# Reordering the start of a fused attention and maxout kernel: loads, casts and copies of batches 0 and 1

## The chip, the cores and the metric

The kernel runs on one core of a Trainium2 chip. The metric is the device time of one execution in microseconds (us); the span that the profile shows is the same execution from first to last instruction, about 1.8 us shorter. PE is TensorE, PEld its weight loads, DVE is VectorE, ACT is ScalarE, POOL is GpSimd, and SPq is the queue from which SyncE issues DMAs. The granted clock is the share of full speed that the profile shows as granted to TensorE (0.978 on the mean in the profiled execution of before).

## The reference, cut to what matters

```python
B, H, S, Ns, D = 8, 8, 512, 32, 64        # x: B,H,S,D   state: B,H,Ns,D
scores = scale * x @ state^T ;  a  = softmax(scores)  ;  xread = a  @ state    # per batch and head
scores2 = scale * state @ x^T;  a2 = softmax(scores2) ;  sread = a2 @ x
X = concat([xread, sread], axis=2) -> [B*(S+Ns), 512]
out = maximum(X @ w1, X @ w2) @ w_out      # w1, w2: 512x1024, w_out: 1024x512
```

The kernel uses two identities. First, max(h1, h2) @ Wo = relu(h1 - h2) @ Wo + h2 @ Wo, so it needs W1 - W2 and the product W2 Wo. Second, xread @ W = a @ (S @ W), so it multiplies the 32 rows of state S by the weights once per batch ("S W", in the buffer `swt`). Layer one of a batch is then `aT` times `swt`.

## The kernel before

Everything of batch 0, and of batch 1 up to its layer one, is a hand-ordered list of calls. From batch 1 on a loop runs layer one and layer two of batch b, and slips the preparation of batch b+1 in between as "fillers". The parts that matter (cuts are marked):

```python
load_x(0)
for ch in range(2): ...                      # W2, Wo
load_w(w1f, moe_w1, 0); load_w(w1f, moe_w1, 1)
load_x(1)
...
def warm_up(n):                              # matmuls on a zero tile, results unused
    p = bank()
    for k in range(n):
        nc.tensor.matmul(p, warm[:, 0:128], warm, start=(k == 0), stop=(k == n - 1))
...
def u_norm(b, g, mul):                       # sum, reciprocal, a = e * 1/sum   (mul: the engine of the last)
    nc.vector.tensor_reduce(d["es"][:, g], ...)
    nc.vector.reciprocal(d["er"][:, g], d["es"][:, g])
    mul.tensor_mul(d["a"][:, g]..., d["e"][:, g], d["er"]...)
def d_at(b):                                 # batches 2..7: aT by DMA transpose
    nc.sync.dma_start_transpose(out=AT[b]..., in_=st[b]["a"]...)
def u_at(b, eng):                            # batches 0, 1: aT on TensorE, copied out of PSUM by eng
    ...
# ---- the list (cut) ----
w_cast(w1b, w1f, 0)                          # W1a (first 512 columns): halves on DVE and ACT
w_sub(0); w_sub(1)                           # W1a - W2a on GpSimd
for i in range(4): w_wo(3, i)                # last group of W2 Wo, copies to wcat within
u_sw(0, 0); u_sw(0, 2)                       # S W of batch 0
l1(0, {}, range(0, 4))
...
u_sc(1, 0, nc.vector)                        # batch 1: scores, exp, norm
u_sc(1, 1, nc.gpsimd)
cast_x(2)                                    # GpSimd
...
u_at(1, "V")
...
one_ring()                                   # PSUM: 4 + 4 buffers become one ring of 8
for b in range(1, B):
    if b + 2 < B: cast_x(b + 2); ...         # GpSimd
    l1(b, fill)
    ...
    l2(b, fill)                              # fillers: ... u_sw(n), d_at(n), d_xt(n + 1), ...
```

The softmax here doesn't subtract the row's maximum and nothing guards it: scores larger than these inputs give would overflow.

## Time and profile before

| | before |
|---|---|
| time, the three executions known when the prediction was made | 156.42 us median, 154.05 to 156.94 |
| profiled execution | 153.81 us, span 152.0, mean granted clock 0.978 |
| layer one of batch 0 starts | 26.77 us |
| scores of batch 1 start | 36.21 us |
| layer one of batch 1 starts | 43.86 us |
| each later batch | 13.96 us |
| PE busy | 142.4 of 152.0 us |

The table says how to read the rest: 108 of the 152 us are a steady march of PE after 43.86 us, and the change works on what lies ahead of it. The prediction below shows the page's rows and the chain. Two more views turn out to matter. The first is the table of windows (window, its length, busy us and instructions of each engine, the granted clock, the DMA share, GB/s):

```profile
8.00:16.00 8.00, 6.86 (x101) 4.96 (x102) 5.88 (x12) 4.65 (x6) 3.04 (x3) 0.57 1.05 389
42.00:50.00 8.00, 7.17 (x55) 3.33 (x54) 4.88 (x9) 3.88 (x9) 2.84 (x3) 1.00 0.88 229
```

In this execution the granted clock was 0.57 from 8 to 16 us. The second is the tile view of `aT`, with the time from the issue of its DMA transpose to its landing, for batches 2 to 7:

```profile
DMA to landing us min/median/max: 3.2/3.3/3.8
```

### The profile page before, as it was taken

What the parts mean: (1) busy time and instruction counts of PE and PEld (TensorE: products, weight loads), DVE (VectorE), ACT (ScalarE), POOL (GpSimd) and SP (SyncE); (2) the same over time, 40 slices, a digit from 0 to 9 for tenths busy, and PEclk for the clock granted to TensorE, in tenths of its full rate; (3) what the DMA queues carried; (4) which work ended last, traced back from release to release, by engine and by line L of the source; (5) the groups of instructions that cost most, each with busy time, mean ns of one, the idle gap of its engine ahead of it and who ended that gap; (6) DMA issues with size and microseconds to landing.
All of it is one profiled execution on the core that took longest, in us unless ns stands there. A gap on an engine that the chain in (4) does not pass through costs nothing.

```text
span 152.0 us, 3031 instructions
## 1 busy us (share of the span) xinstructions
PE 142.4 (94%) x1255; PEld 68.7 (45%) x1255; DVE 85.5 (56%) x151; ACT 75.4 (50%) x126; POOL 44.4 (29%) x44
## 2 busy tenths in 40 slices
PE   6669997999979999999999999999999999999990
PEld 1247462434424544543454445345434534664460
DVE  5366769715965757556654657555566546631120
ACT  3047354845864846374754648463747226621010
POOL 3025329993470460073009003600500050000000
PEclk9965999999999999999999999999999999999999
DMA  4999999939969759939992986593089023602423
GB/s 102 356 393 387 387 383 324 283 80 209 226 129 304 263 107 266 285 107 170 280 297 51 197 296 232 99 246 144 2 107 341 39 35 49 265 0 68 140 100 113
DMA packets 37934, 29.89 MB, mean 197 GB/s; under 512 B 24864, under 2 KB 33312, under 8 KB 37024
## 3 DMA queue, kind: packets, MB, share of 16 engines
q1 hardware_dynamic: 37776, 29.56, 67.9%
q8 instruction: 10, 0.16, 0.4%
q10 hardware_dynamic: 144, 0.13, 0.3%
q14 instruction: 4, 0.03, 0.1%
HBM read 15.20 MB, written 8.91 MB: 159 GB/s over the span
## 4 chain that ended last, share of the span: by engine, by line
PE 84%; DVE 7%; DMA 4%; ACT 2%; issue 0%; SPq 0%
PE acc L326 34%; PE ps L311 18%; PE acc L322 10%; DMA xf<-in_x_dram 4%; PE ps L283 3%; PE ps L221 2%; PE ps L370 2%; PE acc L380 2%; PE acc L415 2%; DVE w1b L70 2%; PE ps L244 2%; PE ps L404 2%; PE acc L360 1%; PE ps L203 1%; PE acc L378 1%; PE ps L136 1%
## 5 line engine op out<-in xcount | busy, mean ns | idle before, releaser
L326 PE MATMUL acc<-wo,r 128*128 128x512 bf16 x248 | 58.9, 379 | 0.0
L326 PEld LDWEIGHTS <-r 128*128 128x128 bf16 x248 | 23.9, 98 | 28.8 <-issue 0.6
L231 POOL TENSOR_TENSOR a<-e,er 128x512 bf16<-128x512 bf16 x13 | 13.4, 1048 | 63.1 <-ACT e L224 29.9
L301 DVE TENSOR_SCALAR r<-ps 128x512 bf16<-128x512 f32 x32 | 22.1, 691 | 16.4 <-PE ps L311 16.3
L311 PE MATMUL ps<-aT,swt 128*128 128x512 bf16 x128 | 29.1, 379 | 1.0 <-ACT sread_t L68 0.8
L70 DVE COPY ob<-acc 128x512 f32<-128x512 f32 (+1 forms) x17 | 11.4, 671 | 27.4 <-PE acc L326 27.0
L299 ACT ACTIVATE r<-ps 128x512 bf16<-128x512 f32 x32 | 19.2, 601 | 8.5 <-PE ps L311 7.9
L68 ACT CAST swt<-ps 128x512 bf16<-128x512 f32 x24 | 12.9, 592 | 14.2 <-PE ps L283 14.2
L311 PEld LDWEIGHTS <-swt 128*128 128x128 bf16 x128 | 12.1, 98 | 15.4 <-DVE swt L70 1.5
L322 PE MATMUL acc<-swt,aT 128*128 128x512 bf16 x62 | 18.1, 381 | 0.0
L68 ACT COPY ob<-acc 128x512 f32<-128x512 f32 (+1 forms) x16 | 9.2, 576 | 15.9 <-PE acc L326 10.9
L70 DVE CAST swt<-ps 128x512 bf16<-128x512 f32 x24 | 15.2, 679 | 1.9 <-PE ps L283 1.9
L72 POOL CAST xp<-xf 128x2048 bf16<-128x2048 f32 (+1 forms) x8 | 14.1, 1761 | 6.3 <-DMA xf<-in_x_dram 6.3
L224 ACT ACTIVATE e<-ps 128x512 bf16<-128x512 f32 x16 | 8.8, 595 | 14.1 <-PE ps L221 14.1
L68 ACT CAST xc<-xf 128x1024 bf16<-128x1024 f32 x14 | 13.9, 1051 | 0.0
L228 DVE TENSOR_REDUCE es<-e 128x16 f32<-128x512 bf16 x16 | 10.6, 662 | 1.6 <-ACT e L224 1.6
L389 POOL TENSOR_TENSOR wcat<-w1f,w2f 128x1024 bf16<-128x1024 f32 x4 | 10.6, 2660 | 2.8 <-DMA w1f<-in_moe_w_dram 2.8
L136 PE MATMUL ps<-warm 128*128 128x512 bf16 x15 | 6.4, 567 | 1.3 <-POOL warm L122 1.3
L322 PEld LDWEIGHTS <-aT 128*128 128x128 bf16 x62 | 4.7, 98 | 6.0 <-issue 2.6
L415 PE MATMUL acc<-wo,w2t 128*128 128x512 bf16 x32 | 7.2, 379 | 0.0
L283 PE MATMUL ps<-wcat,sbd 64*32 64x512 bf16 x168 | 6.8, 380 | 0.2 <-DVE wcat L70 0.2
L221 PEld LDWEIGHTS <-xt 128*128 128x128 bf16 x128 | 5.0, 102 | 2.8 <-ACT xt L68 0.7
(68 smaller groups left out, 107.7 us busy)
## 6 DMA issues: line engine op xcount, KB each, us to landing
xf<-in_x_dram SPq DMA_DIRECT2D x8, 1024.0 KB, 8.7
out_dram<-ob SPq DMA_DIRECT2D x7, 1024.0 KB, 5.1
w2f<-in_moe_w_dram SPq DMA_DIRECT2D x2, 1024.0 KB, 10.4
wof<-in_moe_w_out_dram SPq DMA_DIRECT2D x4, 512.0 KB, 11.1
w1f<-in_moe_w_dram SPq DMA_DIRECT2D x2, 1024.0 KB, 14.3
out_dram<-ob SPq DMA_DIRECT2D x3, 256.0 KB, 2.0
out_dram<-obs SPq DMA_DIRECT2D x8, 64.0 KB, 1.7
s_f<-in_state_dram SPq DMA_DIRECT2D x1, 320.0 KB, 13.3
```

The costliest lines, as they stand in the source:

```text
L68: nc.scalar.copy(o, i)
L70: nc.vector.tensor_copy(o, i)
L72: nc.gpsimd.tensor_copy(o, i)
L228: nc.vector.tensor_reduce(d["es"][:, g], d["e"][:, g].rearrange("p i c n -> p (i c) n"), axis=mybir.AxisListType.X, op=ALU.add)
L231: mul.tensor_mul(d["a"][:, g].rearrange("p c i n -> p i c n"), d["e"][:, g], d["er"][:, g].rearrange("p (i c) -> p i c", i=4).unsqueeze(3) ...
L283: nc.tensor.matmul(pg[g][32 * i:32 * i + 32, :], sneg[gs, b, i, :] if k else sbd[gs, b, 2 * i + g, g, :], w[gs, i, ch * 512:(ch + 1) * 512 ...
L299: nc.scalar.activation(out=o, in_=p, func=ACTF.Relu)
L301: nc.vector.tensor_scalar(o, p, scalar1=0.0, scalar2=None, op0=ALU.max)
L311: nc.tensor.matmul(p, SW[b][:, g, f * 128:(f + 1) * 128], AT[b][:, g, :], start=(g == 0), stop=(g == 1))
L322: nc.tensor.matmul(OB[b][1 + c], AT[b][:, g, c * 128:(c + 1) * 128], SW[b][:, g, FF:WC], start=(g == 0), stop=False)
L326: nc.tensor.matmul(OB[b][1 + c], R[b][:, f, c * 128:(c + 1) * 128], wo[:, f, :], start=False, stop=(f == NF - 1))
L389: nc.gpsimd.tensor_sub(wcat[:, :, cs], w1f[:, :, cs], w2f[:, :, cs])
```

## The change

Its intent is to start layer one of batch 0 earlier, and with it everything behind it. x0 comes in two halves. x1 is loaded ahead of the second half of W1 ("W1b"). W1a is cast by DVE, ACT and GpSimd at once, and the subtraction W1 - W2 moves from that spot to later. S W1 of batch 0 stands right behind the matmuls of W2 Wo, with two of their copies ahead of it and two behind. More warm-up matmuls are meant to keep the clock up (from 8 to 16 us it was 0.57 in the profile of before). For the buffers, two PSUM rings of four stay to the end in place of the later ring of eight. (PSUM holds TensorE's results here, the tiles `ps` and `acc` of the matmul rows; a ring is a set of its buffers, or banks, used in turn.)

```diff
-    early = ctx.enter_context(ExitStack())
-    pools = dict(ps=early..., acc=early...)
+    pools = {k: ctx.enter_context(tc.tile_pool(name=k, bufs=4, space=bass.MemoryType.PSUM)) for k in ("ps", "acc")}
...
-    load_x(0)
+    load_x(0, 2)
...
     load_w(w1f, moe_w1, 0)
+    load_x(1)
     load_w(w1f, moe_w1, 1)
-    load_x(1)
...
-        two = b < TWO and ch < 2 and (b, ch) != (1, 0)
+        two = b < TWO and ch == 0
...
-    warm_up(5)
+    warm_up(9)
...
-    w_cast(w1b, w1f, 0)
-    w_sub(0)
-    w_sub(1)
+    for e, i in (("V", slice(0, 2)), ("A", slice(2, 3)), ("P", slice(3, 4))):
+        copy(e, w1b[:, i, 0:512], w1f[:, i, 0:512])
     for i in range(4):
         w_wo(3, i)
+    w_wo_out(0)
+    w_wo_out(1)
     u_sw(0, 0)
+    w_wo_out(2)
+    w_wo_out(3)
+    cast_x(1)
+    l1(0, {}, range(0, 4))
     u_sw(0, 2)
-    l1(0, {}, range(0, 4))
...
+    w_sub(2, nc.vector)
+    w_sub(3, nc.vector)
...
-    u_sc(1, 0, nc.vector)
-    u_sc(1, 1, nc.gpsimd)
+    u_exp(1, 0)
+    u_exp(1, 1)
+    u_norm(1, 0, nc.vector)
+    u_norm(1, 1, nc.vector)
     cast_x(2)
+    w_sub(0)
+    w_sub(1)
...
-    one_ring()
     for b in range(1, B):
```

(Cut: the order of W2 Wo's groups, of the copies between them and of batch 1's pieces.)

More of the change, by code (lines that the diff above doesn't have):

```diff
@@ L49 @@
     big = ctx.enter_context(tc.tile_pool(name="big", bufs=2))
-    early = ctx.enter_context(ExitStack())
-    pools = dict(ps=early.enter_context(tc.tile_pool(name="ps", bufs=4, space=bass.MemoryType.PSUM)),
-                 acc=early.enter_context(tc.tile_pool(name="acc", bufs=4, space=bass.MemoryType.PSUM)))
+    pools = {k: ctx.enter_context(tc.tile_pool(name=k, bufs=4, space=bass.MemoryType.PSUM)) for k in ("ps", "acc")}
     ctx.enter_context(tc.manual_schedule())
@@ L60, in acc @@
         return bank(kind="acc")
-    def one_ring():
-        early.close()
-        pools["ps"] = pools["acc"] = ctx.enter_context(tc.tile_pool(name="ring", bufs=8, space=bass.MemoryType.PSUM))
     def copy(eng, o, i):
@@ L275, in sw_mm @@
     def sw_mm(b, ch, engs="VA"):
-        pg = [bank(), bank()]
-        two = b < TWO and ch < 2 and (b, ch) != (1, 0)
+        pg = [bank(kind="acc" if ch == 2 and b > 1 else "ps") for g in range(2)]
+        two = b < TWO and ch == 0
         terms = ((sbd, w1b), (sneg, w2b)) if two else ((sbd, wcat),)
@@ L384, in moe_sread, with w_sub @@
                 nc.sync.dma_start(out=out[b * L + S:(b + 1) * L], in_=ob[32 * q:32 * q + 32, t, :])
-    def w_sub(q):
+    def w_sub(q, eng=nc.gpsimd):
         cs = slice(q * 256, (q + 1) * 256)
-        nc.gpsimd.tensor_sub(wcat[:, :, cs], w1f[:, :, cs], w2f[:, :, cs])
+        eng.tensor_sub(wcat[:, :, cs], w1f[:, :, cs], w2f[:, :, cs])
     def w_cast(o, w, ch, engs="VA"):
@@ L415, in w_wo, with w_wo_out @@
             nc.tensor.matmul(WO[i], w2t[:, i, f, :], wo[:, f, :], start=(f == 0), stop=(f == NF - 1))
-        if q == 3:
-            copy("V" if i % 2 else "A", wcat[:, i, FF:WC], WO[i])
+    def w_wo_out(i):
+        copy("V" if i % 2 else "A", wcat[:, i, FF:WC], WO[i])
     def fillers(b):
@@ L444 @@
     states(first)
-    warm_up(5)
-    cast_x(0, (("V", slice(0, 4, 2)), ("A", slice(4, 8, 2)), ("V", slice(1, 4, 2)), ("P", slice(5, 8, 2))))
+    warm_up(9)
+    cast_x(0, (("A", slice(0, 4, 2)), ("V", slice(4, 8, 2)), ("P", slice(1, 4, 2)), ("V", slice(5, 8, 2))))
     u_xt(0, 0, "V")
+    warm_up(2)
     u_xt(0, 1, "A")
     u_exp(0, 0)
+    warm_up(2)
     u_exp(0, 1)
-    w_cast(w2b, w2f, 0, "VV")
+    warm_up(3)
+    w_cast(w2b, w2f, 0, "PA")
+    u_norm(0, 0, nc.vector)
+    u_norm(0, 1, nc.vector)
+    w_t(0, 0, "A")
+    w_t(0, 1, "A")
+    u_sr(0)
     wo_cast(0, "P")
@@ L454 @@
     warm_up(1)
-    w_t(0, 0, "A")
-    w_t(0, 1, "A")
-    u_norm(0, 0, nc.vector)
-    u_sr(0)
-    u_norm(0, 1, nc.vector)
-    negate_states()
-    warm_up(3)
-    for q in range(2):
-        for i in range(4):
-            w_wo(q, i)
+    for i in range(4):
+        w_wo(0, i)
+    u_at(0, "V")
     w_cast(w2b, w2f, 1)
-    wo_cast(2, "P")
+    for i in range(4):
+        w_wo(1, i)
     w_t(1, 0, "V")
     w_t(1, 1, "A")
-    u_at(0, "V")
+    negate_states()
+    wo_cast(2, "P")
+    wo_cast(3, "P")
     u_srt(0)
-    wo_cast(3, "V")
+    warm_up(2)
     for i in range(4):
         w_wo(2, i)
-    w_cast(w1b, w1f, 0)
-    w_sub(0)
-    w_sub(1)
+    for e, i in (("V", slice(0, 2)), ("A", slice(2, 3)), ("P", slice(3, 4))):
+        copy(e, w1b[:, i, 0:512], w1f[:, i, 0:512])
     for i in range(4):
         w_wo(3, i)
+    w_wo_out(0)
+    w_wo_out(1)
     u_sw(0, 0)
+    w_wo_out(2)
+    w_wo_out(3)
+    cast_x(1)
+    l1(0, {}, range(0, 4))
     u_sw(0, 2)
-    l1(0, {}, range(0, 4))
-    for c in range(NC):
-        l2_open(0, c)
-    w_cast(w1b, w1f, 1)
     compact_x(1, 0)
@@ L487 @@
     d_xt(1)
-    cast_x(1)
-    w_sub(2)
-    w_sub(3)
+    load_x(3)
+    w_sub(2, nc.vector)
+    w_sub(3, nc.vector)
     cast_states("P", rest)
-    load_x(3)
     sT = d_states(rest)
-    l2_add(0, 0, range(0, 4))
+    for c in range(NC):
+        l2_open(0, c)
+    for c in range(NC - 1):
+        l2_add(0, c, range(0, 4))
     u_sw(0, 1)
-    for c in range(1, NC):
-        l2_add(0, c, range(0, 4))
+    l2_add(0, 3, range(0, 4))
     l1(0, {}, range(4, 8))
-    u_sc(1, 0, nc.vector)
-    u_sc(1, 1, nc.gpsimd)
+    u_exp(1, 0)
+    u_exp(1, 1)
+    u_norm(1, 0, nc.vector)
+    u_norm(1, 1, nc.vector)
     cast_x(2)
+    w_sub(0)
+    w_sub(1)
     l2_add(0, 0, range(4, 8))
     l2_close(0, 0)
-    u_sw(1, 0)
+    u_sw(1, 1)
+    u_sr(1)
     l2_add(0, 1, range(4, 8))
     l2_close(0, 1)
-    u_sw(1, 1)
-    u_sr(1)
+    u_sw(1, 0)
     compact_x(2, 0)
     compact_x(2, 1)
+    d_xt(2)
     l2_add(0, 2, range(4, 8))
@@ L513 @@
     u_at(1, "V")
+    u_sw(1, 2)
+    u_srt(1)
     l2_add(0, 3, range(4, 8))
     l2_close(0, 3)
-    d_xt(2)
-    u_sw(1, 2)
-    u_srt(1)
     l2_out(0)
-    one_ring()
     for b in range(1, B):
```

## The prediction

> **What bounds the kernel now.** I read the page's busy shares first, then the chain that ended last in order of time, then the timeline of the first 45 us engine by engine, then the groups by shape for durations.
>
> ```profile
> PE 142.4 (94%) x1255; PEld 68.7 (45%) x1255; DVE 85.5 (56%) x151; ACT 75.4 (50%) x126; POOL 44.4 (29%) x44
> ...
> PE   6669997999979999999999999999999999999990
> ...
> PEclk9965999999999999999999999999999999999999
> ```
>
> PE is busy nearly everywhere. The holes lie in the first slices (3.8 us each), and the granted clock is low in slices 2 and 3 (7.6 to 15.2 us). The chain says the same more sharply: from batch 1 on it is PE and nothing else, one batch every 13.96 us.
>
> ```profile
> 43.86 3.62 PE ps L311 x16
> ...
> 57.99 3.45 PE ps L311 x16
> ...
> 71.95 3.45 PE ps L311 x16
> ...
> 85.91 3.45 PE ps L311 x16
> ```
>
> So after 43.86 us, where batch 1's first layer starts, there is nothing to win but the 0.17 us by which the first period (57.99 - 43.86 = 14.13) exceeds the others. Everything hangs on when that point is reached. Before it the chain leaves PE in three places; the lines of the second and third:
>
> ```profile
> 20.87 0.69 DVE aT L70
> 21.56 0.60 DVE wo L70
> 22.16 2.76 DVE w1b L70
> 24.92 1.20 DVE wcat L70 x2
> 26.12 0.61 DVE swt L70
> ...
> 26.77 1.90 PE ps L311 x8
> ...
> 37.28 0.70 DVE es L228
> ...
> 38.98 0.61 DVE es L228
> ...
> 39.87 0.55 DVE ob L70
> 40.41 0.60 DVE swt L70
> ```
>
> The second is 20.87 to 26.73: DVE alone makes W1a's half cast, the copies of W2Wo and of S W1 in a row, and the cast takes 2.8 us. The timeline has why:
>
> ```profile
> 21.73 5.41 POOL L389 TENSOR_TENSOR wcat<-w1f,w2f 128x1024 bf16<-128x1024 f32 x2 [2.82 <-DMA w1f<-in_moe_w_dram]
> ...
> 22.08 2.85 DVE L70 CAST w1b<-w1f 128x1024 bf16<-128x1024 f32 x1
> ```
>
> The third is 37.28 to 43.79: DVE runs without a gap through batch 1's softmax sums and the copies out of PSUM, and batch 1 waits for the last of them. The first, not shown, is 10.39 to 15.31: ScalarE is a chain of its own (xt, two exps, two copies of w2t), after which W2Wo's matmuls start at 15.88 behind three warm-up matmuls.
>
> [...] the same 128x1024 cast costs DVE 0.68 to 0.69 us elsewhere (rows of w1b, w2b, wo) and 2.85 us beside GpSimd's subtraction. [...] GpSimd takes 2.3 to 2.9 us. [...] three warm-up matmuls at 14.76 took 1.28 us (427 ns each), W2Wo's 16 from 16.04 took 3.45 (216 each).
>
> **The change part by part.** Costs are from rows of before: a 128x512 PSUM copy 0.58 us ACT, 0.68 DVE (0.6 start to start); 8 matmuls of 512 columns 1.73; S W for one chunk 0.28, in two terms 0.56.
>
> *Start to 15.2 us.* x0 in two halves lets ACT and DVE cast the first heads at perhaps 6.5 us in place of 8.05, but the second half still lands at 8.03, and xt's second copy stands on ACT. Its chain: xt about 9.9 to 10.9, exps to 12.1, half of w2b (now ACT's, 1.04) to 13.2, w2t twice (1.93) to 15.1. Before, the same chain ended at 15.31. Gain 0.2. In addition 17 warm-up matmuls in place of 9 ahead of W2Wo keep the clock up, and one of them, not three, stands directly in front of it: W2Wo's first group starts with i=0,1 at about 14.3, i=2,3 at 15.2. Gain at this point about 0.7.
>
> *15.2 to l1 of batch 0.* PE in order: rest of the first W2Wo group 0.86, u_at 0.46, second group 1.73, transposes of w2b 1.0, u_srt and two warm-ups 0.65, third and fourth group 3.46: 15.2 + 8.2 = 23.4. W1a cannot land earlier than the 21.65 of before (everything ahead of it in the queue is the same). Its cast: DVE 0.69 for two quarters, ACT about 0.6 and GpSimd 0.5 to 0.86 for one each; [...] it is done by 22.9, beside W2Wo's last group. So S W1 starts on PE at 23.4, takes 0.6, its two copies 0.7 with nothing in front of them (two W2Wo copies come earlier, two later): l1 starts near 24.7, against 26.77. Gain 2.0.
>
> *l1 to the scores of batch 1.* u_sw(0,2) now stands behind l1's first four, and l2_open needs its copy. DVE has l1's fourth relu first (0.69), then the copy (0.68): PE ends u_sw at 26.8 and gets l2_open at 27.8. That is 1.0 us of idle PE that before did not have. Then PE runs through: l2_open 1.73, 12 adds 2.6, u_sw 0.3, 4 adds 0.86, l1 1.73, in all 7.2, so the scores start at 35.1 against 36.24. The subtraction for u_sw(0,1) is on DVE, from W1b's landing at about 27.5 (x1 ahead costs it one megabyte, 24.3 + 3.2)[...]; it is wanted at 32.1. xt of batch 1, 4.5 us behind compact_x's end near 29.6, lands at 34.1. Both off the path. So W1b's second slot loses nothing, and x1's first slot gains nothing beyond that. Gain left: 1.1 to 1.2.
>
> *To batch 1.* DVE's run now starts near 36.1 in place of 37.28. It has one more item: the second multiplication of u_norm moves from GpSimd to DVE (0.69). Before, aT left DVE at 43.20, 5.9 after the run began. Now 5.9 + 0.7, with u_sw(1,2) behind it: aT at 42.8. Before, batch 1 did not start at 43.20 but at 43.86, because the pools changed to one ring there and PE waited for ACT's last copy; that wait goes with the ring. PE's work in this stretch, 5.9 us, ends before DVE's. So batch 1 starts near 42.9: gain 0.95, plus the 0.17 of the first period: 1.1 us.
>
> *After that.* Two rings of four in place of one of eight: per batch 16 tiles of ps and 6 of acc. l1 fills a bank every 0.43 us and two engines empty one each in 0.6 to 0.7; four banks suffice. I count no loss and no gain: 13.96 stays. The end is the same code.
>
> Sum: 1.1 us of the span of 152.0, so 150.9.
>
> **The rivals.** (a) *DVE eats everything.* GpSimd's two subtractions w_sub(0) and (1) now come behind cast_x(2), by my count 32.9 to 37.6, and the two multiplications on DVE (37.1 and 38.6)[...]: up to 0.6 us more. And four ps banks can stop PE: u_sw(1,1), u_sr, u_sw(1,0), u_at and u_sw(1,2) want eight, half of them freed by the engine that is behind. If banks were handed out strictly in turn, u_sw(1,0) would wait for DVE's copy of u_sw(1,1) near 40.6, and batch 1 would start at 43.5 to 44.3: gain 0 or a loss of 0.3. Against it: in before, u_sr ran at 39.51 while DVE had not yet copied u_sw(1,0), at 40.33, so a bank that ACT had emptied was taken. (b) *The clock or the chain of ACT wins more.* If l2_open's wait turns out shorter (relu order) and DVE's run begins at 35, the gain is 2 to 2.3 us: PE's own work from 24.7 to batch 1 is 15.2 us, so the floor is 39.9, and DVE's run cannot reach that. For: PE is idle 1.0 us by my count. Against: DVE's list is fixed. (c) *The DMA queue turns around*: compact_x(2) ends later or xt of batch 2 is late for its scores at 48.4 (4.6 us behind issue, so issue by 43.8). If ACT's two compact casts (2.1 us) come after a stalled u_sw(1,0), it is 0.3 late; otherwise hidden.
>
> **Range and chances.** Relative change: 1.1/154 = 0.7% faster. The three timed runs of before spread from 154.05 to 156.94, so the median of as many is itself good to about 1 us. From 156.42 I get 155.3; the mechanism is good for -0.3 to +2.3 us of gain. Faster by over 2% needs 3.1 us, beyond rival (b), and would need noise; slower by over 2% would need a stall in every batch of the steady part, which I see no cause for.
>
> **What would show it.** L311 of batch 0 (first layer) at 24.7; a DVE w1b cast of about 0.7 to 1.2 us; a PE hole of 1 us ahead of L322's first matmul, released by DVE's swt; DVE without a gap from 36 to 43.5; L311 of batch 1 at 42.9 released by DVE's aT; periods of 13.96 after it; PEclk of 9 in slices 2 and 3. It is wrong if batch 1 starts before 41.5 or after 44.2, or if the period changes.

Statements of how the hardware works that no trace or run of this case shows are cut from it, among them the reason that rival (a) gave for its wait, and with them the estimate for the two subtractions that go to DVE. (The "2.3 to 2.9 us" is what one such subtraction takes on GpSimd.) The forecast's sum: it came to 1.1 us at the start of batch 1 (0.95 there and the 0.17 of the first period), so the span of 152.0 becomes 150.9. What rested on the cut estimate is that the subtraction on DVE is off the path; measured, the two ran from 27.64 to 30.00 us, ahead of the 32.1 at which a result was wanted.

## The result

| | before | after | predicted |
|---|---|---|---|
| time, median of 4 | 155.51 us (154.05 to 156.94) | 159.76 us (159.45 to 159.85) | 155.3 (gain of -0.3 to +2.3) |
| ratio, 95% interval | | 1.0349 (1.0308 to 1.0389) | |
| span of the profiled execution | 152.0 us | 157.7 us | 150.9 |
| layer one of batch 0 starts | 26.77 us | 24.43 us | 24.7 |
| scores of batch 1 start | 36.21 us | 35.07 us | 35.1 |
| layer one of batch 1 starts | 43.86 us | 46.08 us | 42.9 |
| its last matmul starts | 47.10 us | 50.14 us | |
| same point, last batch | 130.86 us | 136.59 us | |

A ratio is the mean time of one kernel's fast executions over that of the other's in the same rounds, so it is not quite the ratio of the quoted medians. An execution counts as slow when it lies over 1.5% above the fastest of the same kernel; of before's four, two do. The changed kernel is slower by 3.5%, where a gain of 0.7% was predicted.

The page of the kernel after has this in place of the rows of before:

```profile
PE 142.7 (90%) x1238; PEld 68.3 (43%) x1257; DVE 86.6 (55%) x150; ACT 75.0 (48%) x126; POOL 41.8 (26%) x44
...
PE   6988995999199998999899989999999999999991
...
PEclk9999999999969999999999999999999999999999
```

PE has as much work as before (142.7 against 142.4 us). The low clock of slices 2 and 3 is gone, as expected. New are a 1 in slice 10 (39.4 to 43.4 us), a 6 in the clock a slice later, and 8s in slices that had 9s.

The timeline of the start (start, us, engine, source line, operation, tiles, and in brackets the idle time before it and what ended it) shows the first steps as predicted. The lines of source are five or six lower here than in before.

```profile
21.84 0.69 DVE L64 CAST w1b<-w1f 128x1024 bf16<-128x1024 f32 x1 [2.48 <-DMA w1f<-in_moe_w_dram]
...
24.43 1.90 PE L306 MATMUL ps<-aT,swt 128*128 128x512 bf16 x8 [0.77 <-DVE swt L64]
```

The timeline from there to batch 1 shows the first loss:

```profile
27.71 1.89 PE L317 MATMUL acc<-swt,aT 128*128 128x512 bf16 x8 [1.04 <-DVE swt L64]
...
34.41 4.68 POOL L384 TENSOR_TENSOR wcat<-w1f,w2f 128x1024 bf16<-128x1024 f32 x2
...
36.14 0.69 DVE L222 TENSOR_REDUCE es<-e 128x16 f32<-128x512 bf16 x1 [0.17 <-ACT e L218]
...
37.14 2.50 DVE L225 TENSOR_TENSOR a<-e,er 128x512 bf16<-128x512 bf16 x1
...
39.63 1.89 POOL L66 CAST xp<-xf 128x2048 bf16<-128x2048 f32 x1 [0.36 <-DMA xf<-in_x_dram]
...
40.55 1.51 DVE L225 TENSOR_TENSOR a<-e,er 128x512 bf16<-128x512 bf16 x1
...
43.32 0.61 PE L256 MATMUL ps<-ident,a 128*128 128x128 bf16 x8 [3.54 <-DVE swt L64]
...
44.38 1.91 PE L321 MATMUL acc<-wo,r 128*128 128x512 bf16 x4
...
46.08 4.43 PE L306 MATMUL ps<-aT,swt 128*128 128x512 bf16 x15
```

In before the first multiplication stood on DVE and the second on GpSimd:

```profile
38.29 0.69 DVE L231 TENSOR_TENSOR a<-e,er 128x512 bf16<-128x512 bf16 x1
...
40.01 1.05 POOL L231 TENSOR_TENSOR a<-e,er 128x512 bf16<-128x512 bf16 x1 [4.29 <-PE ps L244]
```

After the change DVE's run begins at 36.14, as predicted. Then its two multiplications take 2.50 and 1.51 us. One takes 0.69 us when nothing is in its way (the run with the subtractions moved, below, shows both at 0.69). The first ends 0.55 us after GpSimd's pair of subtractions (37.14 + 2.50 = 39.64 against 34.41 + 4.68 = 39.09), the second 0.54 us after GpSimd's cast of x3 (42.06 against 41.52): each time about the multiplication's own time after the end of what GpSimd was doing. DVE is late by 1.81 + 0.82 = 2.63 us. PE sits idle for 3.54 us, and comes back at about half speed: the granted clock is 0.58 from 44 to 46 us and 0.57 from 46 to 48, four matmuls take 1.91 us (1.02 at a clock of 1.00 in e7), and layer one of batch 1 takes 4.43 us in place of 3.62. The last 1.2 us of the hole are not a wait for `a`, which is ready at 42.06: PE's transposes need a PSUM bank, and DVE's copy of S W empties it at 43.27. The window shows the clock:

```profile
42.00:50.00 8.00, 6.58 (x35) 2.95 (x36) 5.71 (x12) 3.13 (x6) 0.00 (x0) 0.79 0.67 173
```

The second loss is in the steady part. The tile view of `aT` now says

```profile
DMA to landing us min/median/max: 3.4/4.4/5.0
```

and the chain that ended last, which was PE alone in before, now has a DMA in it (start, us, what):

```profile
86.32 4.99 DMA aT<-a
91.31 0.04 issue
91.35 1.24 PE ps L306 x5
```

Layer one of batch 4 waits for its `aT`. Three batches do so; the starts of layer one's last matmul are 14.81, 14.62, 15.02, 14.08, 13.96 and 13.96 us apart, where before had 13.96 six times. So the sum of losses is 3.04 us up to batch 1 (50.14 - 47.10) and 2.69 us after it (the excess of the periods over 13.96: 0.85 + 0.66 + 1.06 + 0.12). That makes 5.7 us, as the spans do.

Why did the transposes land late? The DMA view of 58 to 60 us, around the first of the three, has one packet that is no data of the kernel's:

```profile
q8 instruction: 1, 0.02, 2.7%
...
aT<-a SPq DMA_TRANSPOSE x1, 4.9
```

The profile's kind for it is "instruction": a fetch of 16 KB (ten of them, 0.16 MB together, are counted on each page). One comes in every batch, in both kernels. In the packet records of the trace the transpose packets of `aT` run from 57.96 to 59.45 us. The fetch starts at 59.59 and takes 0.88 us. Until about 61.2 us hardly any transpose packets are recorded (about 10 in a quarter of a microsecond in place of 210), and `aT` is complete at 61.7. In the table "fetch" is the start of the 16 KB packet counted from the first transpose packet of that batch's pair (`aT`, then the next `xt`), and "period" is the time to that batch's layer one from the one before:

```
            fetch (us from the first transpose packet)   period (us)
before      +4.03 +4.13 +4.10 +4.17  | -0.39             13.96 in all five
after       +1.63 +1.67 +1.78        | -0.17 -0.52       14.81 14.62 15.02 | 14.08 13.96
```

In before the undisturbed pair takes 4.0 to 4.1 us and the fetch is served just behind it. In after it falls between the two transposes in three batches, and in two others it falls ahead of them. (The last batch's `aT` has no `xt` behind it and is left out.)

**The theories before the experiments.** F (fetch): the fetch, when it falls 1.4 to 1.9 us into the pair, costs that batch up to about 1.1 us, and what places it is the number of TensorE instructions ahead. R (rings): the stalls come from the two rings of four. T (timing): the stalls follow from where the change has put the work in time, above all from batch 1's late start. P ("port theory"; no run shows a port, only who waited): the loss up to batch 1 comes from the subtractions and the cast on GpSimd beside DVE's multiplications.

### The profile page after: what moved, and what is told of

Read it like the earlier page. It is cut to its first block, busy times and chain, and to the rows that moved or that the text cites. A ratio compares the mean times of both kernels' runs of the same rounds, so it can differ in the third digit from the quotient of the medians.

```text
span 157.7 us, 3008 instructions
## 1 busy us (share of the span) xinstructions
PE 142.7 (90%) x1238; PEld 68.3 (43%) x1257; DVE 86.6 (55%) x150; ACT 75.0 (48%) x126; POOL 41.8 (26%) x44
## 5 line engine op out<-in xcount | busy, mean ns | idle before, releaser
L321 PE MATMUL acc<-wo,r 128*128 128x512 bf16 x246 | 59.6, 383 | 0.2 <-issue 0.2
L306 PE MATMUL ps<-aT,swt 128*128 128x512 bf16 x121 | 29.6, 387 | 3.2 <-DMA aT<-a 2.1
L225 POOL TENSOR_TENSOR a<-e,er 128x512 bf16<-128x512 bf16 x12 | 12.3, 1048 | 68.0 <-ACT e L218 43.9
L62 ACT CAST swt<-ps 128x512 bf16<-128x512 f32 x18 | 10.0, 587 | 19.9 <-PE ps L278 19.9
L317 PE MATMUL acc<-swt,aT 128*128 128x512 bf16 x56 | 16.7, 380 | 2.0 <-DVE swt L64 1.0
L64 DVE CAST swt<-ps 128x512 bf16<-128x512 f32 x18 | 11.8, 681 | 3.1 <-PE ps L278 3.1
L130 PE MATMUL ps<-warm 128*128 128x512 bf16 x24 | 8.7, 494 | 1.3 <-POOL warm L116 1.3
L66 POOL CAST wo<-wof 128x1024 bf16<-128x1024 f32 x4 | 4.7, 1164 | 4.4 <-DMA wof<-in_moe_w_out_dram 4.4
L225 DVE TENSOR_TENSOR a<-e,er 128x512 bf16<-128x512 bf16 x4 | 5.7, 1429 | 0.1
```

The costliest lines, as they stand in the source:

```text
L62: nc.scalar.copy(o, i)
L64: nc.vector.tensor_copy(o, i)
L66: nc.gpsimd.tensor_copy(o, i)
L225: mul.tensor_mul(d["a"][:, g].rearrange("p c i n -> p i c n"), d["e"][:, g], d["er"][:, g].rearrange("p (i c) -> p i c", i=4).unsqueeze(3) ...
L306: nc.tensor.matmul(p, SW[b][:, g, f * 128:(f + 1) * 128], AT[b][:, g, :], start=(g == 0), stop=(g == 1))
L317: nc.tensor.matmul(OB[b][1 + c], AT[b][:, g, c * 128:(c + 1) * 128], SW[b][:, g, FF:WC], start=(g == 0), stop=False)
```

## The experiments

Ten runs were made, of nine kernels (e8 and e11 are the same; there is no e9), all with correct results. e1 to e4 ran on one chip, the others on a second, each with executions of before on the same chip. There before had a median of 152.97 us (152.28 to 155.03, nine executions) in e1 to e4, 156.29 (152.44 to 157.29, eleven) in e5 to e8, and 155.51 in e10 and e11 (154.9 to 155.56, four). So the medians of different calls are not to be compared; the ratios are.

### e1: after with two fewer warm-up matmuls

```diff
-    warm_up(9)
+    warm_up(7)
```

> The changed kernel with two warm-up matmuls fewer (four TensorE instructions) in its first warm-up, nothing else. Theory F (the steady part loses 2.7 us because the 16 KB instruction fetch that falls once per batch gets in between the transposes aT and xt and holds aT back; where it falls hangs on the count of TensorE instructions before): with the stream four instructions nearer to that of before the fetches go back behind the transposes, the periods of batches 2 to 4 go from 14.6 to 15.1 back to 13.96, span about 155.0. Rival R (the rings of four banks cause it) and rival T (the late start of batch 1 causes it): no change, 157.5 to 158.1. The start of batch 1 stays near 46 in all.

Measured: 160.76 us (160.43 to 161.39), ratio 1.0534. Layer one of batch 1 starts at 46.02. Five batches stall. The fetches are at +1.42, +1.62, +1.80, +1.89 and +1.73, the periods are 14.54, 14.57, 15.04, 15.14 and 14.94. The direction that F expected did not come: the two instructions moved the fetch the wrong way for me. But two warm-up matmuls at 4.7 us, far from everything, changed the periods at 100 us, and in each batch with a fetch inside the pair the period is long. Neither R nor T has anything that this edit could move.

### e2: after with before's ring of eight from batch 1 on

```diff
-    pools = {... two rings of four ...}
+    early = ...            # as in before
...
+    one_ring()
     for b in range(1, B):
```

> The changed kernel with one ring of eight PSUM banks from batch 1 on, as before. Rival R: the periods go back to 13.96, span 155.0. Theory F: the rings do not matter as such; the wait for the old pools may add up to 0.7 us at the start of batch 1, and the extra wait instructions of TensorE shift the fetches by a few instructions, so the periods may change, but then the fetches must have moved relative to the transposes. Rival T: no change.

Measured: 154.59, 158.51, 157.98 and 159.49 us, so two groups and no ratio. The profile belongs to the first: all periods are 13.96 to 13.99, the fetches lie at +3.98 and +4.07, then at -0.38, -0.62 and -0.93. Layer one of batch 1 started at 44.60, at clock 1.0. R had expected these periods, and F that the fetches would have moved if they came, so this profile does not tell the two apart; e5 and e7 will. The other three executions of the very same program are back at 158 to 159.5. What they looked like inside was not seen.

### e3: after with the subtractions of W1a moved behind batch 1's softmax

```diff
     cast_x(2)
-    w_sub(0)
-    w_sub(1)
...
     # in the loop, b == 1, behind cast_x(3)
+            w_sub(0)
+            w_sub(1)
```

> The changed kernel with the two GpSimd subtractions w_sub(0) and w_sub(1) issued behind the cast of x3 instead of ahead of it. Port theory (the two multiplications of batch 1's softmax on DVE, 2.50 and 1.51 us, stand behind GpSimd's subtractions and cast[...]): they fall back to 0.7 us each, aT leaves DVE near 42.8, batch 1 starts at 42.9 to 43.2 in place of 46.1, TensorE idles under 1.5 us and keeps its clock, span lower by 3.0 to 3.9. If what fills batch 1's late start is DVE's own list of work, under 0.7 us. Theory T of the steady part: with batch 1 early the periods are 13.96 again, in all minus 6; theory F: the periods keep the excess of 2.7 us or change only as the fetches move.

Measured: 155.25 us (154.84 to 155.65), ratio 1.0159, span 153.1. The timeline of DVE:

```profile
36.95 0.69 DVE L225 TENSOR_TENSOR a<-e,er 128x512 bf16<-128x512 bf16 x1
...
38.56 0.69 DVE L225 TENSOR_TENSOR a<-e,er 128x512 bf16<-128x512 bf16 x1
...
41.97 0.68 DVE L64 COPY aT<-ps 128x1024 bf16<-128x1024 bf16 x1
```

Both multiplications are back at 0.69 us, `aT` leaves DVE at 42.65 in place of 45.46, and layer one of batch 1 starts at 42.70, which is the prediction's 42.9 to within 0.2. The clock stays at 1.0. That is P, by taking away its cause. The stalls behind are still there: fetches at +1.46, +1.60 and +1.68 with periods of 14.72, 14.59 and 14.86, then -0.42 and -0.65 with 13.96. So batch 1's lateness is not their cause, and T falls as far as it blames that.

### e4: before with two more warm-up matmuls

```diff
-    warm_up(5)
+    warm_up(7)
```

> The kernel before with two warm-up matmuls more (5 to 7) in TensorE's idle time, so that its later instructions have the same numbers as the changed kernel's. Theory F: the fetches move ahead by four instructions, get in between aT and xt, and some of the periods of batches 2 to 5 grow from 13.96 to 14.6 or more: slower by 0.5 to 3 us. Rivals R and T: same time within 0.3 us.

Measured: 155.20, 153.12, 153.00 and 152.13 us, ratio 1.0 (0.9996). The profile fell in the first, which counts as slow, and has three stalls in the kernel before: fetches at +1.66, +1.77 and 0.01 with periods of 14.93, 15.11 and 14.52, then -0.52 and -0.80 with 13.96. So none of the change is needed for a stall. What the faster three executions looked like was not seen. The profile shows something else too: the clock is 1.00 from 8 to 16 us here, and layer one of batch 0 starts at 24.86, in before's order. W1a landed later in this execution (GpSimd's subtraction starts on it at 22.36, in before at 21.73); from that start to layer one it is 2.50 us, in before 5.04.

### e5: after with warm-up matmuls of half the width and twice the number

```diff
-    def warm_up(n):
-        p = bank()
+    def warm_up(n, kind="ps", w=512):
+        p = bank(kind=kind)
...
-            nc.tensor.matmul(p, warm[:, 0:128], warm, ...)
+            nc.tensor.matmul(p[:, 0:w], warm[:, 0:128], warm[:, 0:w], ...)
...
-    warm_up(9)
+    warm_up(18, w=256)
```

This adds nine matmuls and their weight loads, 18 instructions of TensorE, and no work.

> The changed kernel with its nine warm-up matmuls of 512 columns made 18 of 256, the same work in the same place, 18 TensorE instructions more. The run with four instructions fewer moved the fetches the wrong way (later) and hit five batches. Theory F now: with 18 instructions more every fetch comes before aT's transposes begin, as in batches 6 and 7 of the changed kernel; all periods 13.96, batch 1 still near 46, span 155.0 (minus 2.7). If the fetches are a sign and not a cause, the periods keep 14.6 to 15.1 and the span 157.7.

Measured: 157.57, 155.76, 156.31 and 154.71 us, ratio 1.0128 (1.0022 to 1.0235), unclear by its class. All periods are 13.96, with all fetches ahead of the pair. The tile view of `aT`:

```profile
DMA to landing us min/median/max: 3.0/3.1/3.4
```

The profile is of the slowest execution (span 155.8, mean clock 0.975), and layer one of batch 1 still starts late, at 46.47, so P's loss is whole and F's is gone. e7 below has the same periods in a profile of a fast execution.

### e6: e3 and e5 together

> Both repairs: the two GpSimd subtractions behind the cast of x3, and the 18 warm-up matmuls of half width. The two causes add: batch 1 at 42.7 as in the run with the first repair alone, periods 13.96, span 150.7; against before's undisturbed 152.0 this is 1.3 us less, ratio to before 0.985 to 0.995. If the repairs overlap (the steady stalls only show because of the early part), the span stays over 152.

Measured: 154.33 us (152.74 to 155.48, six executions), ratio 0.9996 (0.9898 to 1.0094). The periods are 13.96. The span of 152.6 missed the expected one because the second multiplication met the cast of x3:

```profile
38.64 1.89 POOL L66 CAST xp<-xf 128x2048 bf16<-128x2048 f32 x1 [1.06 <-DMA xf<-in_x_dram]
...
38.66 2.41 DVE L225 TENSOR_TENSOR a<-e,er 128x512 bf16<-128x512 bf16 x1
```

GpSimd came 0.02 us sooner, and DVE lost 1.72 us. In e3 the multiplication was not held up. The cast waits for a load, so this is a race between a DMA and DVE; the fast executions of this one program lie between 152.74 and 154.38 us.

### e7: after with 14 warm-up matmuls in the idle stretch ahead of `u_at(1)`

```diff
+    warm_up(14, "acc")
     u_at(1, "V")
```

(Here and in e8 `warm_up` takes a kind of bank and a width, as in e5.)

> The changed kernel with 14 warm-up matmuls put into TensorE's idle 3.5 us ahead of batch 1's transposes u_at, in a bank that nobody else wants then. Clock theory (the idle stretch drops the granted clock to 0.57 and the next 5 us run at half speed, 1.4 us lost): the clock stays at 1.0, the second half of layer two and layer one of batch 1 go at 216 ns a matmul, the last matmul of batch 1's layer one starts near 48.7 in place of 50.1. DVE's waits of 2.5 and 1.5 us stay. It adds 28 instructions too, so by theory F the periods fall to 13.96 and the span to about 153.6. If the slow stretch has another cause, the last matmul stays at 50.

Measured: 155.46 us (155.29 to 155.56), ratio 1.0116, span 153.8. PE's timeline:

```profile
39.60 3.19 PE L130 MATMUL acc<-warm 128*128 128x512 bf16 x14
...
45.70 3.61 PE L306 MATMUL ps<-aT,swt 128*128 128x512 bf16 x16
```

The clock in 42 to 50 us is 1.00 in place of 0.79, layer one takes 3.61 in place of 4.43 us, and its last matmul starts at 48.93 in place of 50.14: 1.2 us came from the fallen clock. Layer one still starts late, as DVE's wait is untouched. The 28 more instructions also moved the fetches out of the pair, and the periods are all 13.96.

### e8 and e11: before with its warm-up matmuls at half the width and twice the number

```diff
-    warm_up(5)
+    warm_up(10, w=256)
...
-    warm_up(1)
+    warm_up(2, w=256)
...
-    warm_up(3)
+    warm_up(6, w=256)
```

> The kernel before with its warm-up matmuls but the first six halved in width and doubled in number, nine more, 18 instructions. By theory F the runs of before that take 155 us are those in which the fetches fall between aT and xt; with the fetches well ahead of the transposes no run does: all runs within 152 to 153, median 0 to 0.5 us under that of before, span 152.0 or a little less. If before's spread has another cause, some of the runs are at 155 again.

> The kernel before with split warm-ups once more, on the chip of the run above, to set the two side by side and to see whether its narrow spread (151.7 to 152.8 in six runs) repeats: all runs within 151.5 to 153, while before itself spreads to 155 or 157. If a run is at 155 or more, the account of before's spread by the place of the fetches is not whole.

Measured: e8 151.95 us (151.72 to 152.8, six executions), ratio 0.9898 (0.984 to 0.9957); e11, the same kernel, 151.82 us (151.64 to 152.51, six), ratio 0.9782 (0.9743 to 0.9822). The ratios differ because before itself differed; the kernel with split warm-ups did not. Before covered 152.4 to 157.3 us on that chip, this one 151.6 to 152.8 in twelve executions. All fetches lie ahead of the pair and all periods are 13.96.

The profile, at a clock of 1.00 from 8 to 16 us, has something on the start too:

```profile
21.84 0.69 DVE L70 CAST w1b<-w1f 128x1024 bf16<-128x1024 f32 x1 [2.02 <-DMA w1f<-in_moe_w_dram]
...
21.89 5.16 POOL L389 TENSOR_TENSOR wcat<-w1f,w2f 128x1024 bf16<-128x1024 f32 x2 [3.05 <-DMA w1f<-in_moe_w_dram]
...
24.39 1.89 PE L311 MATMUL ps<-aT,swt 128*128 128x512 bf16 x8
```

With before's own order, layer one of batch 0 starts at 24.39, as early as in the changed kernel (24.43). DVE reaches the cast 0.05 us before GpSimd starts its subtraction, where in before it came 0.35 us after it, and the cast takes 0.69 in place of 2.85 us.

### e10: both losses taken out of the changed kernel, and its two known holes closed

On top of e6, the second multiplication goes back to GpSimd, the cast of x2 is issued before it, and the second S W chunk of batch 0 comes two pieces of layer one earlier:

```diff
-    l1(0, {}, range(0, 4))
+    l1(0, {}, range(0, 2))
     u_sw(0, 2)
+    l1(0, {}, range(2, 4))
...
+    cast_x(2)
     u_exp(1, 0)
     u_exp(1, 1)
     u_norm(1, 0, nc.vector)
-    u_norm(1, 1, nc.vector)
-    cast_x(2)
+    u_norm(1, 1, nc.gpsimd)
```

> The changed kernel with the late subtractions and the split warm-ups, and two repairs more: the second multiplication of batch 1's softmax back on GpSimd (its queue: cast of x2, multiplication, cast of x3, so that no cast can come between), and u_sw(0,2) between the second and third piece of layer one, so that its copies do not stand behind the fourth relu. If the hole of 1.04 us ahead of l2_open and DVE's list are what still separates the changed kernel from before with split warm-ups (batch 1 at 44.5 in the last run, 42.7 in a run without the collision, 41.8 there), batch 1 starts at 41.2 to 41.9, span 149.4 to 150.2, faster than before by 1 to 3 per cent. If it stays at 42.5 or more, the rings of four or the arrival of xt bound it.

Measured: 151.07 us (150.97 to 151.18, six executions), ratio 0.9728 (0.9704 to 0.9753), span 149.2. It beats both kernels, and e11 of the same call by 0.75 us in the medians. Which of the two added repairs gave how much was not run apart. Its chain:

```profile
26.72 1.89 PE acc L317 x8
...
41.11 3.61 PE ps L306 x16
```

The hole of 1.04 us ahead of the layer-two opening is gone (26.72 in place of 27.71), and layer one of batch 1 starts at 41.11, 5 us ahead of the changed kernel and 0.7 us ahead of e8 and e11 (41.78, 41.81). All periods are 13.96. Its six executions lie within 0.2 us.

### The fetch in all profiles

```
            fetch at                          period
e1          +1.42 +1.62 +1.80 +1.89 +1.73     14.54 14.57 15.04 15.14 14.94
e3          +1.46 +1.60 +1.68 | -0.42 -0.65   14.72 14.59 14.86 | 13.96 13.96
e4          +1.66 +1.77 0.01 | -0.52 -0.80    14.93 15.11 14.52 | 13.96 13.96
e2          +3.98 +4.07 | -0.38 -0.62 -0.93   13.96 to 13.99 in all
e5 e6 e7 e8 e10 e11   all -0.83 to -1.56      13.96 in all
```

With before and after, a fetch that starts +1.4 to +1.9 us into the pair goes with a period of 14.5 to 15.1 us in 13 of 13 cases. One that starts at +3.98 or later, or at -0.38 or sooner, goes with 13.96 to 13.99 in every case. Between them lie two: 0.01 with 14.52, and -0.17 with 14.08.

## Why the prediction was wrong

**Start to layer one of batch 0: the place right, the gain not.** 24.7 was predicted and 24.43 measured, in part by luck: S W1 started on PE at 22.61 in place of the 23.4 counted, and then took 1.05 us in place of 0.6, as GpSimd's quarter of the cast took 1.14 us in place of 0.5 to 0.86. "Gain 2.0" was measured from a profile of before that fell in an execution with a clock of 0.57 from 8 to 16 us. At a clock of 1.00 there, before's order with other warm-ups starts layer one at 24.86 (e4), 24.39 (e8) and 24.53 (e11), each time 2.5 us after GpSimd can start on W1a, where the changed kernel takes 2.6. So against such a baseline the reordered casts gain nothing here. It goes on to batch 1: these three start its layer one at 42.49, 41.78 and 41.81, all ahead of the predicted 42.9, so that start, come true, would have been no gain over them. Of before itself no execution with a full clock was profiled.

**Layer one to the scores: right.** The hole predicted at 1.0 us is 1.04 us, released by DVE's copy as said. The scores start at 35.07 (35.1 predicted), DVE's run at 36.14 (36.1). The two subtractions on DVE took 2.36 us together, 1.18 each.

**The step "To batch 1" failed.** It said "Now 5.9 + 0.7, with u_sw(1,2) behind it: aT at 42.8." `aT` left DVE at 45.46. Rival (a) had named the place, "the two multiplications on DVE" beside GpSimd's subtractions, and mis-sized the term: "up to 0.6 us more" measured 2.63 us. There were two reasons. The count had the subtractions ending at 37.6; they ended at 39.09, because the cast of x2 ahead of them waited for its load until 32.56. And the second multiplication met the cast of x3 of the loop, which the working did not have at all. In these three cases the multiplication ended 0.54 to 0.55 us after the GpSimd instruction beside it, so it cost about what was left of that instruction, not a share: 1.95, 0.97 and (e6) 1.87 us were left, and the multiplication took 2.50, 1.51 and 2.41 us, which is 1.81, 0.82 and 1.72 longer than its 0.69. What in the hardware makes it wait, the runs do not show. e3 confirms the size: with the subtractions gone from there, batch 1 started at 42.70. Rival (a)'s other half, that four banks can stop PE, came true for the last 1.2 us of PE's hole; as DVE had no gap before `aT`, it did not hold `aT` up.

**A term that the sum did not have: the clock.** The wait left PE idle for 3.54 us, and the granted clock fell (0.79 from 42 to 50 us): four matmuls took 1.91 us. The prediction had read such a slow stretch off before's warm-ups (427 ns a matmul, 216 later) and did not count one here. e7 measures the term at 1.2 us, by keeping PE busy in the hole.

**The step "After that" failed.** "I count no loss and no gain: 13.96 stays." The first four periods were 14.81, 14.62, 15.02 and 14.08, in sum 2.69 us too long. The rings, which that step argued about, are not the cause: e5 and e7 keep two rings of four and have 13.96. What goes with every stall is an instruction fetch that falls between the two DMA transposes, after which `aT` lands late. e1 and e5 move it both ways: a change of nothing but the warm-up instructions, at 4.7 us, makes the stalls worse or takes them away. e4 has it in the kernel before, in a slow execution. That the fetch itself holds the packets up, and not something else that moves with it, rests on this and on the order of the packets.

The 0.17 us that the prediction counted for the first period was a misreading of the chain. A piece of the chain starts where the piece before it ends, and that was 57.99; the first matmul of batch 2's layer one starts at 57.83, which is 13.97 after 43.86. There was nothing to win.

"Slower by over 2% would need a stall in every batch of the steady part, which I see no cause for" was thus wrong twice: three batches were enough beside the loss at batch 1, and stalls did come.

The sum, against the predicted span of 150.9: 3.2 us for the start of batch 1 (46.08 - 42.9; DVE's wait of 2.63, the rest in part the slow matmuls ahead of it), 0.8 for layer one on the low clock (from its first matmul's start to its last's 4.06 us in place of 3.24), the 0.17 us of the first period, and 2.7 for the fetches. That is 6.9; measured 6.8 (157.7 - 150.9).

**The spread of before.** The prediction took the spread of 154.05 to 156.94 for noise. It is at least not the clock alone: four executions of before, all with a mean clock of 1.000, had spans of 150.7, 151.9, 155.0 and 155.2. Splitting the warm-ups in e8 and e11 made the spread 1.2 us. Since the fetch's place decides a microsecond per batch, it is a likely source, but no long execution of before itself was profiled; only e4's was.

**What stays open.** That the fetch is TensorE's is inferred, not shown: its packets come once per batch of 258 TensorE instructions, and edits to TensorE's instructions alone moved them. What triggers it, how far ahead of execution it is made, and why before's fetches were served behind both transposes where after's came between them, the runs do not tell. Nor do they tell why `aT`, whose packets had nearly all run by 59.45 us, landed only at 61.4 to 61.7, when the fetch's packet had ended at 60.47. The number of instructions may not be all that places it: executions of one program lie 5 us apart in e2 and 3 us in e4 (there at mean clocks of 0.995 to 1.0). I could move the fetch with warm-ups, but e1's direction was a miss, so I could not aim it.

## What to carry to other kernels

Before moving an instruction to DVE, list everything that GpSimd does in the same stretch, including what the next loop iteration issues there. Charge what is left of the GpSimd instruction, not a fraction: here the multiplication lost 1.81 us where 1.95 were left, 0.82 of 0.97 and 1.72 of 1.87. Which of the two comes first can change from run to run when one side waits for a load: DVE's cast took 0.69 us when it came 0.05 us ahead of GpSimd (e8) and 2.85 us when it came 0.35 us behind (before), and GpSimd's 0.02 us cost 1.72 us in e6. Then ask what the idle time that follows on PE does to its clock: after 3.54 us of it the changed kernel had 0.79 from 42 to 50 us, after 2.09 us e2 had 1.00. When a steady period grows though nothing in the loop changed, look at the instruction queue among the DMA packets: a few more or fewer instructions at the start may shift a fetch into or out of a critical transfer (four fewer at 4.7 us made it five stalls in place of three in e1, 18 more left none in e5). Profile more than one execution of the baseline, above all when its times spread by more than the gain that is sought.
